# Second pair of heads turned and compared while the first pair's clusters are found, and the table of exponentials loaded early

## The chip, the cores and the metric

The kernel runs on one core of a Trainium2 chip. The metric is the device time of one execution in microseconds (us). The kernel before took 892.93 us, the median of four runs (891.25 to 893.72).

## What is computed

Two blocks, one after the other. The first is a routed attention over q, k and v of shape (4, 8, 768, 64): four batches, eight heads, 768 rows, 64 columns. Each row of q and of k is assigned to one of 16 clusters, whose centroids are given for each head, and a query sees only the keys of its own cluster:

```
q_assign = argmax(q_n @ c_n)              # over 16 clusters; k_assign likewise
mask   = q_assign[..., :, None] == k_assign[..., None, :]
scores = where(mask, q @ k.T / sqrt(64), -1e9)
attn   = softmax(scores)
x      = attn @ v                         # then (batch, row) x (head, column): 3072 x 512
```

The second block is a mixture of experts: each of the 3072 rows of x goes to the one of eight experts with the largest logit of `x @ w_gate`, through `relu(x @ w1[e]) @ w2[e]` (512 to 1024 to 512), and the result is scaled by the softmax weight of the chosen expert. Everything is in float32.

## The kernel before, in words

The attention works on 16 groups, each of them a pair of heads of one batch; group 0 is the first pair, group 1 the second. For one group the steps are functions of the kernel:

- `load` (L506): SyncE issues five transfers, two for q, two for k, one for v. q and k have two buffers each, v has three.
- `turn` (L570): TensorE turns q and k, 12 transposes of 128 x 128, eight in the first piece and four in the second, each piece into one PSUM tile of the ring `sps` (three tiles). VectorE scales q out of PSUM (L582), then ScalarE copies what k there is (L583), and later the second piece (L585).
- `similar` (L587): TensorE compares all rows with the centroids (L592, eight matmul instructions into the single PSUM tile `mps`, four of them on q and then four on k), and ScalarE copies the result out (L597). `similar2` (L599) turns it back with three transposes (L603), and ScalarE copies it out (L605).
- `assign` and `assign2` (L607, L616): the largest of 16, with ties going to the first: VectorE (L611, L612), GpSimd (L613), VectorE (L619, L620).
- `put` (L625): TensorE turns the one-hot rows (L630, 12 transposes in bfloat16, again into a tile of `sps`); ScalarE copies those of q out (L634), then VectorE those of k (L635).
- `score` (L645), 12 for a group: two products of q and k (L652) with the product of the one-hot rows added to them in PSUM (L655), which drives the scores of other clusters far down; ScalarE takes the exponential (L657), and VectorE adds up the sums for the softmax (L660, L664).
- `attend` (L666), 12 for a group: the exponentials times v (L672), summed up in the PSUM tile `O`.

`finish`, `weigh`, `x_turn`, `gate` and `keep_rows` then make the rows of x and the logits. The experts follow at the end; a few of their steps are begun during the attention.

The order on every engine is written out by hand: each engine runs its instructions strictly in the order in which the program issues them. That order is set by turns. In turn n the program issues three scores, then the jobs entered for (n, 0), then the three attends of the turn before, then the jobs for (n, 1). A group has four turns (TG = 4). The line `at(n - 4, 0, turn, g, 0)` and those after it (L776 to L782) enter a group's preparation in the four turns ahead of its first score, n = 4g. So group 0 is prepared in turns -4 to -1, in which there is no score, and group 1 in turns 0 to 3, beside the scores of group 0.

Before all this, at L519 to L565, the centroids and the gate's weights are loaded on ScalarE's queue, groups 0 and 1 on SyncE's queue (L522, L523), and the centroids are normalised: ScalarE squares them (L544) and takes a root (L546), VectorE and TensorE do the rest. A function of ScalarE that isn't in the table at hand is preceded by a load of another table. GpSimd makes constants there, and more of them in turn 1 (`place_consts`, L358).

Of the kernel before, what the change touches and what calls it, by code (L numbers as in the profile page):

```python
# [12 lines left out]
AF = mybir.ActivationFunctionType  # L13
# [170 lines left out]
def kernel(  # L184
# [11 lines left out]
    nc = tc.nc  # L196
# [4 lines left out]
    HP = H // 2  # L201
# [28 lines left out]
    def fetch(e, i):  # L230
        i %= 3
        w1 = wpools[i].tile([P, DB, F], F32, name=f"w1_{i}")
        w2 = wpools[i].tile([P, FB, Dm], F32, name=f"w2_{i}")
        nc.sync.dma_start(out=w1, in_=moe_w1[bass.ds(e, 1)].rearrange("e (a p) f -> p (e a) f", p=P))
        nc.sync.dma_start(out=w2, in_=moe_w2[bass.ds(e, 1)].rearrange("e (a p) d -> p (e a) d", p=P))
        return w1, w2
# [255 lines left out]
    with ExitStack() as actx:  # L492
# [11 lines left out]
        rows = {}  # L504

        def load(g):  # L506
            b, hp = divmod(g, HP)
            for name, src in (("q", q), ("k", k)):
                t = rows[g, name] = ld.tile([P, NQ, 2, D], F32, name=name + "_in")
                for a in range(2):  # L510
                    nc.sync.dma_start(out=t[:, :, a, :], in_=src[b, 2 * hp + a].rearrange("(p j) d -> p j d", j=NQ))
            t = rows[g, "v"] = ld.tile([P, 2, NQ, D], F32, name="v_in", bufs=3)
            nc.sync.dma_start(
                out=t.rearrange("p a j d -> p a (j d)"),
                in_=v[b, 2 * hp : 2 * hp + 2].rearrange("a (p j) d -> p a (j d)", j=NQ),
            )
# [2 lines left out]
        nc.scalar.dma_start(out=csb, in_=centroids.rearrange("h c d -> (h c) d"))  # L519
        wg_in = consts.tile([P, DB, E], F32)  # L520
        nc.scalar.dma_start(out=wg_in, in_=moe_w_gate.rearrange("(a p) e -> p a e", p=P))
        load(0)  # L522
        load(1)  # L523
        make_identity(nc, ident)
        nc.vector.tensor_copy(ident_b, ident)
        first_c = iota("first_c", [P, C], [[-1, C]], C, 0)
# [15 lines left out]
        csq = consts.tile([P, D], F32)  # L542
        cs2 = consts.tile([P, 1], F32)
        nc.scalar.activation(csq, csb, AF.Square, accum_out=cs2)  # L544
        cnrm = consts.tile([P, 1], F32)
        nc.scalar.activation(cnrm, cs2, AF.Sqrt)  # L546
        cinv = consts.tile([P, 1], F32)
        nc.vector.tensor_scalar_max(cinv, cnrm, 1e-30)
        nc.vector.reciprocal(cinv, cinv)
# [215 lines left out]
        def at(n, part, f, *a):  # L765
            jobs.setdefault((n, part), []).append((f, a))
# [6 lines left out]
        at(1, 1, place_consts)  # L773
        for g in range(NG):
            n = g * TG
            at(n - 4, 0, turn, g, 0)  # L776
            at(n - 4, 1, turn, g, 1)
            at(n - 3, 0, similar, g)
            at(n - 3, 1, similar2, g)
            at(n - 2, 0, assign, g)  # L780
            at(n - 2, 0, assign2, g)
            at(n - 1, 0, put, g)  # L782
            at(n + TH, 1, finish, g, 0)
            at(n + 2 * TH, 1, finish, g, 1)
            if g < NG - 1:
                at(n + TG + 2, 0, weigh, g)
                at(n + TG + 2, 1, weigh2, g)
                at(n + TG + 3, 1, x_turn, g, 0)
                at(n + TG + 4, 0, x_turn, g, 1)
                if g % HP == HP - 1:  # L790
                    at(n + TG + 3, 0, gate, g // HP)
                    at(n + TG + 4, 0, keep_rows, g // HP)
# [39 lines left out]
        n = (NG - HP) * TG  # L832
# [10 lines left out]
        n = NG * TG  # L843
# [8 lines left out]
        for g in range(2, NG):  # L852
            at((g - 2) * TG + 1, 0, load, g)
# [23 lines left out]
    with tc.tile_pool(name="sm", bufs=1) as sm:  # L877
# [21 lines left out]
        for part in parts:  # L899
            n, over = part["n"], part["over"]  # L900
# [84 lines left out]
    with tc.If(nx > XU):  # L985
        with tc.For_i(XU, nx, 1) as i:
# [4 lines left out]
            g = dict(n=[P], rows=N, w=fetch(ex, 0), gi=lambda j: gi[:, 0:1], si=lambda j: gi[:, 1:2], apart=False)  # L991
# [36 lines left out]
```

## Time and profile before

| what | value |
|---|---|
| median of four runs | 892.93 us |
| the profiled execution | 891.28 us, of which its span 889.4 us |
| TensorE matmul busy | 840.0 us (94%) |
| VectorE, ScalarE, GpSimd busy | 316.0, 263.3, 107.7 us |
| mean granted clock of TensorE | 0.984 |
| first matmul of the program | 7.19 us from the span's start |
| first score (L652) | 18.71 us |
| first score of turn 2 | 31.49 us |

The span runs from the first instruction to the last; what the device time has beyond it lies around the program. All times of single instructions are counted from the span's start. The stretch that the change touches is the first 40 us: the load and normalisation of the centroids, then group 0 from its transposes to its first scores, then turns 0 to 3.

In the views, PE is TensorE's matmuls, PEld its loads of weights, DVE is VectorE, ACT is ScalarE, POOL is GpSimd and SP is SyncE. In a row of the timeline stand the start, the duration, the engine, the line, the operation, what is written and what is read, and in brackets how long the engine was idle before and what ended that. A float32 matmul shows as two instructions or more.

### The profile page before, as it was taken

How to read it: one execution, taken by the hardware profiler on the slowest of the kernel's cores; microseconds unless marked ns; L12 is line 12 of the kernel's file. 1: busy time of each engine (PE TensorE's matmuls, PEld its weight loads, DVE VectorE, ACT ScalarE, POOL GpSimd, SP SyncE). 2: the span in 40 equal slices, each digit the busy share in tenths (PEclk: the TensorE clock that was granted, in tenths of full speed). 3: DMA queues.
4: the chain of work that ended last, by engine and by line, in shares of the span. 5: the costliest groups of instructions: out<-in, count | busy, mean ns of one | idle time of the engine just before them, and what ended most of it. 6: DMA issues, size and time to landing. Idle time of an engine off the chain costs nothing.

```text
span 889.4 us, 10764 instructions
## 1 busy us (share of the span) xinstructions
PE 840.0 (94%) x4397; PEld 438.0 (49%) x4397; DVE 316.0 (36%) x559; ACT 263.3 (30%) x401; POOL 107.7 (12%) x165
## 2 busy tenths in 40 slices
PE   4999999999999999999987899999999999999994
PEld 2444454544445454444655645645344444545462
DVE  2555556556555657756252101010101020200000
ACT  3554555455555555554200110110010101001010
POOL 3000000000000000220024120302020302001010
PEclk8999999999999999999998999999999999999998
DMA  7126321372242201210421144423242422313010
GB/s 161 36 55 223 73 54 64 64 242 54 54 125 55 52 21 35 90 37 1 189 84 39 41 163 171 155 111 143 107 145 99 165 96 81 141 67 109 24 37 7
DMA packets 76186, 81.69 MB, mean 92 GB/s; under 512 B 52831, under 2 KB 56927, under 8 KB 75616
## 3 DMA queue, kind: packets, MB, share of 16 engines
q1 hardware_dynamic: 70208, 60.82, 22.2%
q0 software_dynamic: 5248, 20.04, 6.3%
q8 instruction: 37, 0.61, 0.3%
q14 instruction: 21, 0.17, 0.1%
q10 hardware_dynamic: 672, 0.05, 0.1%
HBM read 68.26 MB, written 13.68 MB: 92 GB/s over the span
## 4 chain that ended last, share of the span: by engine, by line
PE 45%; issue 39%; POOL 7%; DVE 5%; ACT 1%; POOLq 0%; ACTq 0%; DVEq 0%
PE sps L652 14%; PE O L672 13%; PE mps L690 3%; PE sps L655 3%; POOL out_dram L307 3%; POOL xg L270 3%; PE sps L292 3%; PE sps L578 3%; DVE T L664 2%; PE sps L733 1%; PE mps L592 1%; PE sps L630 1%; POOL oh_c L459 1%; PE mps L603 1%; PE sps L336 1%
## 5 line engine op out<-in xcount | busy, mean ns | idle before, releaser
L292 PE MATMUL sps<-xgT,w 128*128 128x416 f32 (+2 forms) x640 | 176.8, 437 | 0.7 <-issue 0.7
L657 ACT ACTIVATE A<-sps 128x768 f32<-128x768 f32 x192 | 154.7, 812 | 68.6 <-PE sps L655 67.6
L652 PE MATMUL sps<-qk 64*128 64x384 f32 x768 | 164.4, 503 | 1.4 <-ACT qk L583 1.0
L336 PE MATMUL sps<-w,h_sb 128*128 128x512 f32 x368 | 160.6, 595 | 1.3 <-DVE h_sb L300 0.9
L292 PEld LDWEIGHTS sps<-xgT,w 128*128 128x128 f32 x640 | 112.2, 192 | 67.7 <-issue 50.6
L664 DVE TENSOR_TENSOR T<-T,A 128x768 f32<-128x768 f32 x128 | 122.5, 957 | 49.1 <-ACT A L657 39.4
L672 PE MATMUL O<-A,v_in 128*64 128x384 f32 x768 | 138.0, 494 | 0.0
L300 DVE TENSOR_SCALAR h_sb<-sps 128x416 f32<-128x416 f32 (+2 forms) x34 | 18.7, 550 | 317.9 <-PE sps L292 317.9
L336 PEld LDWEIGHTS sps<-w,h_sb 128*128 128x128 f32 x368 | 69.1, 190 | 92.4 <-issue 90.5
L652 PEld LDWEIGHTS sps<-qk 64*128 64x128 f32 x768 | 68.1, 188 | 36.9 <-issue 32.6
L306 ACT ACTIVATE zo<-sps,xg 128x512 f32<-128x512 f32 (+1 forms) x34 | 23.3, 685 | 204.5 <-PE sps L336 195.5
L672 PEld LDWEIGHTS O<-A,v_in 128*64 128x64 f32 x768 | 49.4, 136 | 69.8 <-issue 68.4
L307 POOL DMA_INDIRECT out_dram<-zo,s_idx x34 | 33.2, 977 | 351.1 <-ACT zo L306 334.0
L655 PE MATMUL sps<-ohT 64*128 64x384 bf16 x384 | 66.2, 324 | 2.2 <-DVE ohT L635 2.2
L302 ACT ACTIVATE h_sb<-sps 128x416 f32<-128x416 f32 (+2 forms) x34 | 16.5, 484 | 166.5 <-DVE h_sb L300 166.5
L660 DVE SCALAR_TENSOR_TENSOR T<-A 128x768 f32<-128x768 f32 x32 | 30.7, 958 | 84.0 <-ACT A L657 84.0
L613 POOL TENSOR_TENSOR sim<-sim,first_c 128x384 f32<-128x384 f32 x16 | 16.0, 997 | 292.6 <-DVE sim L612 292.6
L270 POOL DMA_INDIRECT xg<-x_rows,g_idx x34 | 33.3, 980 | 25.5 <-DVE xe L940 10.8
L655 PEld LDWEIGHTS <-ohT 64*128 64x128 bf16 x384 | 22.2, 94 | 27.3 <-DVE ohT L635 6.0
L280 PE MATMUL sps<-ident,xg 128*128 128x128 f32 (+1 forms) x136 | 18.4, 266 | 11.2 <-DVE xgT L281 11.2
L680 ACT COPY xT<-O 128x384 f32<-128x384 f32 x32 | 15.4, 481 | 31.4 <-PE O L672 31.4
L690 PE MATMUL mps<-T,one_row 128*32 128x384 f32 x128 | 23.7, 492 | 0.0
(190 smaller groups left out, 541.3 us busy)
## 6 DMA issues: line engine op xcount, KB each, us to landing
w<-in_moe_w_dram SPq DMA_DIRECT2D x20, 2048.0 KB, 9.4
x_rows<-x POOLq DMA_DIRECT2D x4, 1548.0 KB, 6.7
q_in<-in_q_dram SPq DMA_DIRECT2D x32, 192.0 KB, 4.5
k_in<-in_k_dram SPq DMA_DIRECT2D x32, 192.0 KB, 4.9
v_in<-in_v_dram SPq DMA_DIRECT2D x16, 384.0 KB, 3.4
xg<-x_rows,g_idx POOLq DMA_INDIRECT x34, 5.0
out_dram<-zo,s_idx POOLq DMA_INDIRECT x34, 3.3
csb<-in_centroids_dram ACTq DMA_DIRECT2D x1, 32.0 KB, 1.7
```

Of the source, the lines that this page charges most:

```text
L270: nc.gpsimd.indirect_dma_start(out=g["xg"][0:m, j, :], out_offset=None, in_=x_d[0 : g["rows"], :], in_offset=bass.IndirectOffsetOnAxis(ap= ...
L292: nc.tensor.matmul(o, lhsT=g["w"][0][:, c, fb * P : (fb + 1) * P], rhs=g["xT"][:, c, :cols], start=(c == 0), stop=(c == DB - 1),)
L307: ins = nc.gpsimd.indirect_dma_start(out=out[:, :], out_offset=bass.IndirectOffsetOnAxis(ap=g["si"](j)[0:m], axis=0), in_=zo[0:m], in_offs ...
L336: nc.tensor.matmul(zp, lhsT=g["h"][:, fb, j * P : (j + 1) * P], rhs=g["w"][1][:, fb, :], start=(fb == 0), stop=(fb == FB - 1),)
L578: nc.tensor.transpose(ps[:, i * P : (i + 1) * P], rows[g, "qk"[w]][:, j].rearrange("p a d -> p (a d)"), ident)
L652: nc.tensor.matmul(ps[:, a, 0:HS], lhsT=qk[g][r, 1, ks], rhs=qk[g][r, 0, qs], start=True, stop=False)
L655: nc.tensor.matmul(ps[:, a, 0:HS], lhsT=ohT[g][r, 1, ks], rhs=ohT[g][r, 0, qs], start=False, stop=True)
L657: nc.scalar.activation(A[u], ps[:, :, 0:HS], AF.Exp)
L660: nc.vector.scalar_tensor_tensor(T[g, half], in0=A[u - 1], scalar=1e-9 / P, in1=A[u], op0=ALU.add, op1=ALU.add)
L664: nc.vector.tensor_tensor(T[g, half], T[g, half], A[u], op=ALU.add)
L672: nc.tensor.matmul(O[g, half][a * D : (a + 1) * D, 0:HS], lhsT=rows[g, "v"][:, a, j, :], rhs=a_[:, a, :], start=(j == 0), stop=(j == NQ - 1),)
L690: nc.tensor.matmul(ps[half * 32 : (half + 1) * 32, 0:HS], lhsT=one_row[:, i, :] if i < 2 else wg[:, g % HP, :], rhs=t[half][:, i, :] if i ...
```

## The change

It has four parts.

1. `load` is split into `load_qk` and `load_v`. For groups 0 and 1 the transfers are issued in the order q and k of group 0, q and k of group 1, v of group 0, v of group 1. The later loads keep their order.
2. After the root of the centroids' norms ScalarE gets one more activation: an Exp of the 128 x 1 norms into a column of `csq` that nobody reads any more.
3. `turn` and `similar` of group 1 are entered in turn -2, after `assign` and `assign2` of group 0, and `similar2` of group 1 in turn -1, after `put` of group 0. They were in turns 0 and 1.
4. `assign`, `assign2` and `put` of group 1 stay in turns 2 and 3, and all other groups stay where they were.

```diff
         def load(g):
+            load_qk(g)
+            load_v(g)
+
+        def load_qk(g):
             b, hp = divmod(g, HP)
             for name, src in (("q", q), ("k", k)):
...
+        def load_v(g):
+            b, hp = divmod(g, HP)
             t = rows[g, "v"] = ld.tile([P, 2, NQ, D], F32, name="v_in", bufs=3)
...
-        load(0)
-        load(1)
+        for f in (load_qk, load_v):
+            for g in range(2):
+                f(g)
...
         nc.scalar.activation(cnrm, cs2, AF.Sqrt)
+
+        nc.scalar.activation(csq[:, 0:1], cnrm, AF.Exp)
...
         for g in range(NG):
             n = g * TG
-            at(n - 4, 0, turn, g, 0)
-            at(n - 4, 1, turn, g, 1)
-            at(n - 3, 0, similar, g)
-            at(n - 3, 1, similar2, g)
+            if g == 1:
+
+                for f, a in ((turn, (g, 0)), (turn, (g, 1)), (similar, (g,)), (similar2, (g,))):
+                    at(-1 if f is similar2 else -2, 1, f, *a)
+            else:
+                at(n - 4, 0, turn, g, 0)
+                at(n - 4, 1, turn, g, 1)
+                at(n - 3, 0, similar, g)
+                at(n - 3, 1, similar2, g)
             at(n - 2, 0, assign, g)
             at(n - 2, 0, assign2, g)
             at(n - 1, 0, put, g)
```

## The prediction

> **What bounds the kernel now.** I read the engine shares and the slices of the page first, then the chain that ended last within the first 40 us, then the timeline and the half-microsecond windows there. The page says that TensorE is busy nearly everywhere:
>
> ```profile
> PE 840.0 (94%) x4397; PEld 438.0 (49%) x4397; DVE 316.0 (36%) x559; ACT 263.3 (30%) x401; POOL 107.7 (12%) x165
> PE   4999999999999999999987899999999999999994
> ```
>
> Only the first slice and the last stand at 4. What shortens the start before the dense part therefore comes off the end one for one, and so does TensorE work that is taken out of the dense part and put into an idle stretch. TensorE's waits after the start are short (the longest is 2.2 us, for oh_c at L459) and none is for a load, so I see nothing later that would swallow a shift. The chain of the first 40 us (start, length, engine, line) shows both sides of the change:
>
> ```profile
> 13.35 0.49 ACT sim L605
> ...
> 16.70 0.57 DVE oh L620
> 17.27 0.05 issue
> 17.32 1.46 PE sps L630 x12
> 18.78 1.58 PE sps L652 x4
> ...
> 25.00 0.88 DVE qk L582
> 25.88 0.02 issue
> 25.90 0.38 ACT qk L583
> 26.28 0.04 issue
> 26.32 0.92 PE sps L652 x4
> ...
> 28.21 0.78 PE mps L592 x8
> 28.99 2.09 PE O L672 x12
> 31.08 0.48 PE mps L603 x3
> 31.55 0.85 PE sps L652 x4
> ```
>
> From 13.3 to 17.3 the cluster choice of group 0 goes through ACT, DVE and POOL and TensorE has nothing: 4.01 us. From 22.83 on it turns and compares group 1 between scores. The timeline adds who waits, in square brackets:
>
> ```profile
> 10.37 0.37 ACT L583 COPY qk<-sps 128x256 f32<-128x256 f32 x1 [5.51 <-DVE qk L582]
> 17.32 1.46 PE L630 MATMUL sps<-ident_b,oh 128*128 128x128 bf16 x12 [4.01 <-DVE oh L620]
> 19.63 1.28 ACT L657 ACT_TABLE_LOAD   x1
> 22.83 0.87 PE L578 MATMUL sps<-ident,q_in 128*128 128x128 f32 x6
> 26.32 0.92 PE L652 MATMUL sps<-qk 64*128 64x384 f32 x4 [0.96 <-ACT qk L583]
> ```
>
> The windows give the granted clock in the third figure from the right:
>
> ```profile
> 14.50:15.00 0.50, 0.00 (x0) 0.00 (x0) 0.50 (x1) 0.00 (x0) 0.00 (x0) 0.85 1.30 216
> 21.50:22.00 0.50, 0.50 (x6) 0.23 (x4) 0.00 (x0) 0.24 (x1) 0.00 (x0) 0.82 0.00 0
> ```
>
> Between them it is 0.50. So it fell at 14.85 (0.7 of that half at full speed), 1.5 us after the last matmul of 13.3, and rose at 21.68: 6.83 us at half speed.
>
> **The change part by part.** I count to one point that is the same in both programs: the start of score 6 (turn 2), at 31.49 before. The rest keeps its order, so its shift is the result.
>
> *What leaves the dense part.* From turns 0 and 1 go the 12 transposes (22.83 to 24.29, 1.46 us), the 0.96 us wait for their PSUM tile to be copied out, the comparison L592 (0.78 in the chain) and the three transposes L603 (0.48): 3.68 us.
>
> *Where it goes.* On TensorE's queue the order becomes: L603 of group 0 (ends 13.31), transposes of group 1, L592 of group 1, the transposes L630 of group 0, L603 of group 1, score 0. The transposes find TensorE idle and the clock still up: 12 x 0.145 (six took 0.87) = 1.75, from 13.35 to 15.1, free. But the copy L582 out of PSUM stands on DVE's queue behind L619 and L620 of group 0, which wait for POOL. It starts when L620 ends, about 17.2 (at 24.92 it overlapped the tail of its predecessor too), takes 0.95 and ends at 18.16. ACT's copy L583 follows it as at 10.37 and 25.90, and L585 ends 0.86 later (10.37 to 11.23): 19.04. L592 of group 1 needs these copies, and **L630 of group 0 is queued behind it on TensorE**. That is the new wait: L630 now waits for a DVE copy of the next group and for eight matmuls, and behind it stand all scores.
>
> *Price of that wait.* The second half of L592 can load at 19.08. In group 0 that half ran at nearly full speed: loads at 11.28, end at 12.18, 0.90 us. For half speed there is no row. Two passes start 0.32 apart at full speed, which makes 0.64 at half: 0.09 + 2 x 0.64 + 0.2 = 1.6 us. So L592 ends at 19.98 or at 20.7; its streaming is over some 0.18 earlier. L630 took 1.46 at half speed, and 0.84 at full speed (at 64.43). Then come ACT's copy L634 (0.04 + 0.80), DVE's L635 (0.03 + 0.56) and 0.05 to the first L655, by the rows at 18.82 and 19.65.
>
> *Which clock.* First-half matmuls of L592 took 849 ns and the last 487 ns, so the clock first rose between 10.5 and 11.7. Steps at 11.44, 14.85, 18.26 and 21.68, one each 3.41 us, fit all three changes (an estimate from these rows). Before, TensorE was busy for about 1.3 of the 3.4 us up to 14.85 and lost the clock; the transposes now fill 13.35 to 14.85, so it should hold there. Up to 18.26 TensorE is busy only until 15.1, so it falls there and returns at 21.68. I take half speed for L592 and L630, as this is nearest to the row at 14.85: streaming over at 20.5, L630 to 21.93, L634 to 22.76, L635 to 23.35, L655 of score 0 at 23.40. Before it was 20.26: 3.14 us late.
>
> The Trainium skill (TensorE: Matmul & The Clock Gate, "What's actually happening") has the array go cold only after a whole idle window of about 3.4 us. By that rule the 3.2 us gap from 15.1 to 18.3 would often cost no clock, and the sum would be that of the first rival below; but the same rule would not have let the clock fall at 14.85, 1.5 us into a gap, so I follow the row.
>
> *What comes back.* Scores 0 and 1 ran at half speed before (L655 at 20.26 and 21.77, 1.51 apart); after 21.68 they run 0.81 apart (43.32, 44.13, 44.94). So L655 of score 5 is at 23.40 + 5 x 0.81 = 27.45, the attends start 0.26 later and take 2.09: score 6 starts at 29.80. ACT keeps up: an exp is 0.81 too, and the PSUM tile of score u is read 0.6 us before score u+3 wants it. **31.49 - 29.80 = 1.69 us gained.** (As a balance: 3.68 out, 3.14 lost at score 0, and some 1.2 of half-speed scores saved.)
>
> *The table.* The 1.28 us load at 19.63 stands before the first exp, but L655 of score 0 ended at 20.76 and the exp began at 20.93: it was worth 0.17 at most, and the next exp waited for TensorE at 22.13 anyway. I take 0; at most 0.17 is gained. The early load and a one-column exp (1.28 + 0.2, from 4.87 to 6.4) lie in ACT's 5.51 us of idleness before 10.37; uncovered they would cost 1.5. Without the move the load would now meet L605 of group 1 on ACT before exp 0, up to 0.8, so it protects the gain rather than adds one.
>
> *SyncE's queue.* The four q and k loads of group 1 pass v of group 0: v's issue goes from 3.61 to about 7.2 (1.23 + 2.40 of issuing), and with some 4.7 us to landing it is there by 12, against 27.7 when it is first read. Group 1's q and k were issued by 8.19 and, at 4.6 to landing, there by 12.8, so they were in time for 13.35 even without the reorder: nothing gained. Group 3's q and k, which waited 10.1 us for the transposes until 23.73, can go at about 14; they are needed late, and v of group 3 waits for the attends in both. POOL's constants (16.0 to 21.0) are not moved.
>
> The profiled execution took 891.28: a span of 889.4 and 1.9 around it. It becomes 889.6. The median of the four runs is 1.65 above it, so on the median I forecast 892.93 - 1.69 = **891.24**. What one measurement can tell from no change is about 0.2%, 1.79 us, so this lies right at the edge.
>
> **The rivals.**
>
> *A, the clock does not fall.* For it: the new gap is 3.2 us instead of 4.0, and where the steps fall against the program need not be the same in each run. Against it: 14.85. L592 then ends at 19.98, L630 runs from 19.8 to 20.65, L655 of score 0 comes at 22.13: 1.27 sooner, 2.96 gained, 889.97.
>
> *B, one more stretch at half speed.* For it: L592 uses 32 columns and may be too little work to raise the clock at 21.68; for other positions of the steps, too, the kernel before would have had one slow score less. Then L630 ends 0.2 later, and scores 0 and 1 are 1.51 apart instead of 0.81: 1.69 - 0.2 - 0.7 = 0.8 gained, 892.1.
>
> *C, slower: half speed until about 32.* One mechanism, at the scores of turns 0 and 1: the clock returns three steps late. L655 of scores 0 to 5 come at 23.5, 25.0, 26.5, 28.0, 29.5 and 31.0, the attends end at 33.9: 2.4 us lost, 895.3. It decides from a return at about 30 on. For it: at 18.26 the clock did not return although TensorE had just started again. Against it: by 21.68 TensorE had been busy without a break and it returned.
>
> *D, the change does nothing.* Only the reorder of loads and the table alone would give this (0 to 0.17); the moved matmuls are queue order and can't be hidden.
>
> **How the numbers follow.** Forecast 0.52, its own range 890.6 to 891.9 (gains of 1.0 to 2.3, for other positions of the clock steps and the bounds of L592): 0.23 of it is over 1.79, 0.29 under. A 0.23, faster. B and D 0.15, same. C 0.10, slower. Faster 0.46, same 0.44, slower 0.10. Left out of the range are C and the outer tenth: it goes from A's 889.97 less 0.4, 889.6, to B's 892.1 plus 1.2, 893.3 (a single run of the kernel before lay up to 1.7 from the median, most of them less than 1).
>
> **What would show it.** Right: transposes of group 1 from 13.35 to 15.1; L582 of group 1 at 17.2, right after L620; L630 near 20.5 with L592 before it; L655 of score 0 near 23.4 and score 6 near 29.8; no table load near 20; a clock of 1.00 at 15 and 0.50 from 18.3 to 21.7. Wrong: L630 still at 17.3, or L655 of score 0 beyond 25.1, where the gain is gone; a later wait of TensorE for a load would refute the one-for-one shift.

## The result

The changed kernel takes 889.56 us, the median of 48 runs, against 892.74 us for the kernel before (76 runs); the ratio is 0.9973, with a 95% interval of 0.9967 to 0.9979. It is faster by 0.27%, some 2.4 us. The two medians are 3.2 us apart; the ratio goes with the means, 892.14 and 889.73. The forecast was 1.69 us (0.19%). On the forecast's own base of 892.93 us the ratio gives 890.5: inside its whole range (889.6 to 893.3), just below the 890.6 to 891.9 of its main case.

The lines of the changed kernel stand lower in the file by 10: the copy out of PSUM L582 is now L592, the comparison L592 is L602, the transposes of the one-hot rows L630 are L640, and L652 and L655 are L662 and L665. In this document score 0 is the first of a group's twelve scores, score 6 the first of turn 2. The page of the changed kernel, engine shares and slices:

```profile
PE 839.5 (95%) x4397; PEld 438.0 (49%) x4397; DVE 315.5 (36%) x559; ACT 263.2 (30%) x402; POOL 107.5 (12%) x165
PE   4999999999999999999987899999999999999994
```

The work is the same; only its place has moved. The timeline of the changed kernel shows the place (start, length, engine, line; in brackets the idle time before and what ended it):

```profile
13.20 0.82 PE L588 MATMUL sps<-ident,q_in 128*128 128x128 f32 x6
13.85 0.82 PE L588 MATMUL sps<-ident,k_in 128*128 128x128 f32 x6
...
16.17 0.55 DVE L629 TENSOR_REDUCE top<-sim 128x24 f32<-128x384 f32 x1 [1.11 <-POOL sim L623]
...
16.75 0.56 DVE L630 TENSOR_TENSOR oh<-sim,top 128x384 bf16<-128x384 f32 x1
...
17.23 0.95 DVE L592 TENSOR_SCALAR qk<-sps 128x768 f32<-128x768 f32 x1
...
18.33 2.29 PE L602 MATMUL mps<-qk,cblk 128*32 128x384 f32 x8 [3.65 <-DVE qk L592]
...
20.55 1.46 PE L640 MATMUL sps<-ident_b,oh 128*128 128x128 bf16 x12
...
23.50 0.34 PE L665 MATMUL sps<-ohT 64*128 64x384 bf16 x2
...
29.89 0.92 PE L662 MATMUL sps<-qk 64*128 64x384 f32 x4
```

The transposes of group 1 fill what was idle. Their copy L592 follows L630 on DVE, the comparison L602 waits for it for 3.65 us, and L640 of group 0, which before ran at 17.32, runs behind L602 at 20.55. The first one-hot product of score 0 (L665) is late by 3.24 us, and score 6 nevertheless starts at 29.89 instead of 31.49: 1.60 us sooner. The windows of the changed kernel date the clock's steps (the third figure from the right; the last two rows are for later):

```profile
14.50:15.00 0.50, 0.17 (x2) 0.00 (x0) 0.50 (x1) 0.00 (x0) 0.00 (x0) 1.00 1.35 221
16.00:17.00 1.00, 0.00 (x0) 0.00 (x0) 0.80 (x2) 0.00 (x0) 0.91 (x6) 1.00 1.12 321
18.50:19.00 0.50, 0.50 (x4) 0.00 (x0) 0.00 (x0) 0.50 (x2) 0.43 (x4) 0.89 1.36 219
22.00:22.50 0.50, 0.50 (x6) 0.28 (x4) 0.00 (x0) 0.45 (x1) 0.00 (x0) 0.70 0.00 0
...
470.00:472.00 2.00, 1.57 (x11) 1.57 (x11) 0.73 (x5) 0.00 (x0) 1.42 (x2) 0.50 0.00 0
774.00:776.00 2.00, 2.00 (x12) 0.39 (x8) 0.00 (x0) 0.00 (x0) 0.00 (x0) 0.50 1.02 422
```

It is at half speed from 18.89 to 22.30, one stretch of 3.41 us where the kernel before had 6.83. One step of 3.41 us before 18.89 lies 15.47, and there it held: at 16 to 17 us it is still 1.00, with TensorE idle.

The shift of 1.6 us is still there at the last token matmul (472.4 before, 470.8 after), but the spans differ by 2.3 us (889.4 and 887.1). The other 0.7 lies behind it, in a stretch that the change doesn't touch. Two windows of the kernel before, at 494 and 626 us:

```profile
494.00:496.00 2.00, 2.00 (x6) 1.43 (x5) 0.00 (x0) 0.00 (x0) 0.00 (x0) 0.50 0.02 4
626.00:628.00 2.00, 2.00 (x12) 0.44 (x12) 0.24 (x1) 0.00 (x0) 0.00 (x0) 0.50 1.03 420
```

The last two windows of the changed kernel above, at 470 and 774 us, are of the same kind. Both kernels run at half speed for a while at the token matmuls (6.8 us before, 10.2 after, which cost the changed kernel 1.1) and in single stretches of 3.4 us among the experts: two before (492.7 to 496.1, 625.8 to 629.2), one after (773.2 to 776.6). One such stretch costs 1.7: from their first matmul to the end of the last the experts take 386.1 us with two and 384.4 with one. Two stretches against one, less the 1.1, make 0.6 of the 0.7.

### The profile page after: what moved, and what is told of

It is laid out like the page before. It is cut to its first block, busy times and chain, and to the rows that moved or that the text cites. A ratio compares the mean times of both kernels' runs of the same rounds, so it can differ in the third digit from the quotient of the medians.

```text
span 887.1 us, 10766 instructions
## 1 busy us (share of the span) xinstructions
PE 839.5 (95%) x4397; PEld 438.0 (49%) x4397; DVE 315.5 (36%) x559; ACT 263.2 (30%) x402; POOL 107.5 (12%) x165
## 4 chain that ended last, share of the span: by engine, by line
PE 46%; issue 39%; POOL 7%; DVE 5%; ACT 1%; DMA 0%; POOLq 0%; ACTq 0%; DVEq 0%
PE sps L662 14%; PE O L682 13%; PE mps L700 3%; PE sps L665 3%; POOL out_dram L307 3%; POOL xg L270 3%; PE sps L292 3%; PE sps L588 3%; PE mps L602 2%; DVE T L674 2%; PE sps L743 1%; PE sps L640 1%; POOL oh_c L459 1%; PE sps L336 1%; PE mps L613 1%
## 5 line engine op out<-in xcount | busy, mean ns | idle before, releaser
L662 PE MATMUL sps<-qk 64*128 64x384 f32 x768 | 162.9, 499 | 0.5 <-DVE x L746 0.5
L662 PEld LDWEIGHTS sps<-qk 64*128 64x128 f32 x768 | 67.7, 186 | 35.9 <-issue 33.2
L665 PE MATMUL sps<-ohT 64*128 64x384 bf16 x384 | 66.0, 323 | 2.3 <-DVE ohT L645 2.0
L665 PEld LDWEIGHTS <-ohT 64*128 64x128 bf16 x384 | 22.1, 94 | 26.8 <-DVE ohT L645 5.7
L292 PE MATMUL sps<-xT,w 128*128 128x128 f32 x192 | 24.6, 295 | 0.0
```

The costliest lines, as they stand in the source:

```text
L292: nc.tensor.matmul(o, lhsT=g["w"][0][:, c, fb * P : (fb + 1) * P], rhs=g["xT"][:, c, :cols], start=(c == 0), stop=(c == DB - 1),)
L662: nc.tensor.matmul(ps[:, a, 0:HS], lhsT=qk[g][r, 1, ks], rhs=qk[g][r, 0, qs], start=True, stop=False)
L665: nc.tensor.matmul(ps[:, a, 0:HS], lhsT=ohT[g][r, 1, ks], rhs=ohT[g][r, 0, qs], start=False, stop=True)
```

## The experiments

In all of them two readings are used. The first is the start of score 6 counted from the first transpose of group 0's similarities (L603 before, L613 after). That removes what comes earlier, since this transpose itself starts anywhere between 12.13 and 13.12 in the eleven experiments, in kernels of both kinds: at 12.59 on average in the eight profiles with the move, at 12.60 in the five without it. It is 18.73 before (31.49 - 12.76) and 17.08 after (29.89 - 12.81). The second is the median.

### One part of the change alone

```diff
# e1: the changed kernel without its loads' order and its early Exp
# e6: the kernel before with only this
+        nc.scalar.activation(csq[:, 0:1], cnrm, AF.Exp)
# e7: the kernel before with only this
-        load(0)
-        load(1)
+        for f in (load_qk, load_v):
+            for g in range(2):
+                f(g)
```

> Only the four functions of group 1 are moved; the loads keep their old order and the table of exponentials is loaded before the first exp as before. Theory 1 (queue account: 3.7 us leave the dense part, 3.1 are lost because L630 of group 0 stands behind L582 and L592 of group 1, 1.2 come back from scores at full speed): the move is the whole gain. The table load falls after the copy of sim on ACT, at about 23.2, so that the first exp comes at 24.5 instead of 23.9, which the PSUM ring hides but for 0 to 0.4 us; score 6 at 29.9 to 30.3, median 889.6 to 890.2. Theory 2 (the table is what counts, 1.28 us on the path): score 6 at 31.2 and a median of 890.9 or more.

> The kernel before with the early Exp alone. Theory 1: the first exp comes 0 to 0.2 us sooner, nothing else moves; equal to the kernel before within 0.2 us. Theory 2 (the table counts 1.28 us): 1.3 us faster.

> The kernel before with q and k of group 1 loaded ahead of v of group 0, alone. Theory 1: nothing waits for these loads; equal to the kernel before within 0.2 us, with score 6 near 31.5. Theory 6 (the first matmul of the program, at 6.68 with the change against 7.19 before, came sooner because of the order of loads): first matmul at 6.7 and 0.5 us faster.

Measured: e1 889.8 us, ratio 0.9981 (0.9967 to 0.9994); e6 891.09, ratio 1.0 (0.9986 to 1.0013); e7 890.98, ratio 0.9998 (0.9984 to 1.0013). Score 6 stands at 29.46, 30.40 and 30.96. The move is the gain. The table's load and the order of the loads, each alone, are not distinguishable from nothing, which ends theory 2; theory 6 ends too, because e7, with the new order of loads, starts its first matmul at 7.17, and e1, with the old one, at 6.87. In e1 the load of the table falls where it was expected (e1's line numbers are lower by 3 than those of the changed kernel):

```profile
22.59 1.28 ACT L664 ACT_TABLE_LOAD   x1
...
23.89 3.62 ACT L664 ACTIVATE A<-sps 128x768 f32<-128x768 f32 x5
...
24.75 0.30 PEld L659 LDWEIGHTS sps<-qk 64*128 64x128 f32 x4 [0.51 <-ACT A L664]
```

The first exp ends later, so score 3 waits for its PSUM tile until 24.75; at the distance of the scores around it, it would have started at 24.63. Its one-hot product also follows 0.75 us after it instead of 0.64. From the one-hot product of score 0 to score 6 e1 takes 6.62 us (22.84 to 29.46) and the changed kernel 6.39, both at full clock, so by these profiles the early table is worth 0.23 us inside the move. That e1 needs 17.08 us from the transpose to score 6 all the same goes with its clock, which came back 0.89 us sooner after the transpose.

e6 and e7 also show what was not expected: counted from the transpose, score 6 comes after 18.07 and 18.28 us, with the same instructions that took 18.73 in the profile before. In both the clock was down for 3.4 us only, not for 6.8. So the start of the kernel before has no single length; the 1.60 of one pair of profiles is 1.0 to 1.65, counted from the transpose, over these three.

### The wait of the one-hot transposes

```diff
# e2: the changed kernel, the comparison of group 1 behind the one-hot transposes of group 0
-                    at(-1 if f is similar2 else -2, 1, f, *a)
+                    at(-2 if f is turn else -1, 1, f, *a)
# e3: instead, the second half of group 0's choice behind group 1's comparison
+                    if f is similar:
+                        at(-2, 1, assign2, 0)
...
-            at(n - 2, 0, assign2, g)
+            if g:
+                at(n - 2, 0, assign2, g)
```

> As the changed kernel, but L592 of group 1 stands behind L630 of group 0 on TensorE instead of ahead of it. Theory 1: L630 runs at 17.4 instead of 20.55; ACT's copy of it waits behind the two copies L593 and L595 of group 1 until 19.1, so the first L665 comes at 22.1 (after L602 of group 1 and its transposes, which still stand ahead of score 0), 1.4 us sooner than 23.50; median 888.2. Theory 3 (the wait of L640 is not what delays score 0, as ACT and DVE would be late anyway): no gain over the changed kernel, 889.6.

> As the changed kernel, but the second half of the cluster choice of group 0 (L619 and L620 of the kernel before) is entered after the move of group 1, so that DVE copies group 1's q out of PSUM while GpSimd multiplies, instead of behind it. Theory 1: the copy runs from 15.0 to 16.0 in DVE's idle 1.1 us, L602 of group 1 from 16.1 to 17.7, L640 of group 0 at 17.6 at full speed, the first L665 at 19.9 instead of 23.50, score 6 at 26.3 instead of 29.9; median 886.0. Theory 3 (DVE's order is not the cause of the delay): the first L665 within 0.5 us of 23.5, median 889.6.

In e2 L640 starts at 16.89, at once after the cluster choice, and the first L665 at 22.00 (22.1 expected). Score 6 comes 16.05 us after the transpose, 1.03 less than in the changed kernel. The twelve executions fall apart, six at 885.7 to 887.8 and six at 891.4 to 894.3, so that the median, 889.55, says nothing; the ratio is 0.998 (0.9958 to 1.0002). The trace shows the wait removed; the times don't show a gain.

In e3 the copy runs on DVE while GpSimd multiplies:

```profile
14.93 0.95 DVE L592 TENSOR_SCALAR qk<-sps 128x768 f32<-128x768 f32 x1
...
16.02 1.64 PE L602 MATMUL mps<-qk,cblk 128*32 128x384 f32 x8 [1.40 <-DVE qk L592]
16.12 0.55 DVE L629 TENSOR_REDUCE top<-sim 128x24 f32<-128x384 f32 x1 [0.25 <-POOL sim L623]
...
17.59 0.84 PE L640 MATMUL sps<-ident_b,oh 128*128 128x128 bf16 x12
...
19.92 0.34 PE L665 MATMUL sps<-ohT 64*128 64x384 bf16 x2 [0.23 <-DVE ohT L645]
```

DVE's wait for GpSimd falls from 1.11 to 0.25 us, L602 is nearly over when L640 wants the array, and TensorE's gap shrinks to 1.40 us, so that the clock never falls: L602 takes 1.64 and L640 0.84. Score 6 starts at 26.31 (26.3 expected), 13.54 us after the transpose, 3.54 less than with the change. The median is 886.58 (886.0 expected), the ratio 0.9946 (0.9927 to 0.9964). Theory 3 is out: the place of one DVE copy in its queue is what held score 0 up. The 3.54 us hold two things, since the shorter gap also keeps the clock up: 1.26 is the clock by e5 below, and the other 2.28 (15.82 - 13.54, both at full clock) the place in the queue.

### The clock at the start

```diff
# both: n transposes of the identity into a PSUM tile that nobody reads
+        def spin(n):
+            ps = wide().rearrange("p a c -> p (a c)")
+            for i in range(n):
+                nc.tensor.transpose(ps[:, i % 8 * P : (i % 8 + 1) * P], ident, ident)
# e4: the kernel before
+        at(-2, 1, spin, 26)
# e5: the changed kernel
-                for f, a in ((turn, (g, 0)), (turn, (g, 1)), (similar, (g,)), (similar2, (g,))):
+                for f, a in ((turn, (g, 0)), (turn, (g, 1)), (spin, (19,)), (similar, (g,)), (similar2, (g,))):
```

> The kernel before, with 26 transposes of the identity added on TensorE between 13.3 and 17.1, into a PSUM tile that nobody reads, so that only the clock changes. Theory 1: the clock stays at full speed; L630 takes 0.84 instead of 1.46, scores 0 and 1 follow each other after 0.81 instead of 1.51 except where the table load holds the first exp; score 6 at 30.2 instead of 31.49, median 891.4 (1.3 less). Theory 4 (the whole gain of the change is the clock that its transposes keep up): score 6 at 29.9 and a median of 889.6, as with the change itself. Theory 5 (transposes do not count as work for the clock): no change, 892.7, with the clock at 0.50 from 14.9 on.

> The changed kernel, with 19 transposes of the identity added on TensorE between the transposes of group 1 and L602 of group 1 (15 to 18 us), into a PSUM tile that nobody reads. Theory 1 (half speed for L602 and L640 is a term of the loss at score 0, as forecast in rival A): the clock stays at 1.00, L602 takes 1.64 instead of 2.29, L640 0.84 instead of 1.46, the first L665 comes at 22.1 instead of 23.50 and score 6 at 28.6 instead of 29.89; median 888.2. Theory 4 (the clock at the start is not on the path, as the copies of ACT and DVE are late anyway): score 6 unmoved, 889.6.

The timeline of e5:

```profile
14.44 2.24 PE L776 MATMUL sps<-ident 128*128 128x128 f32 x19
...
18.27 1.64 PE L602 MATMUL mps<-qk,cblk 128*32 128x384 f32 x8 [1.60 <-DVE qk L592]
...
19.85 0.84 PE L640 MATMUL sps<-ident_b,oh 128*128 128x128 bf16 x12
...
22.17 0.34 PE L665 MATMUL sps<-ohT 64*128 64x384 bf16 x2 [0.23 <-DVE ohT L645]
```

The clock is 1.00 from 11.73 on through the whole start, the first L665 comes at 22.17 (22.1 expected), score 6 at 28.56, 15.82 after the transpose. Half speed had cost the changed kernel 17.08 - 15.82 = 1.26 us. The median is 888.57, the ratio 0.9967 (0.9954 to 0.9981).

In e4 score 6 comes 17.61 us after the transpose, so half speed had cost the kernel before 0.46 to 1.12 in the three profiles of its kind. At 30.73 it misses the expected 30.2: score 4 still waits 1.13 for the copies of group 1 out of PSUM, which I had not carried over. The median is 890.84, the ratio 0.9995 (0.998 to 1.0009). Theory 5 is out, as the clock stays at 1.00 on transposes alone; theory 4 is out as well: keeping the clock up in the kernel before does not give what the change gives. At full clock on both sides the change is worth 17.61 - 15.82 = 1.79 us, which is the order of the queues (and the early table) without the clock.

### The stretches beyond 470 us

```diff
# e8: e3, and a filler of five after each row tile at the experts' borders
# e9, e10, e11: e4, e5 and e3, and a filler of five only where j is even
+            if spins and j % 2 == 0 and j + 1 < len(g["n"]):
+                sp = ps_m.tile([P, 512], F32, name="mps")
+                for i in range(spins):
+                    nc.tensor.transpose(sp[:, i % 4 * P : (i % 4 + 1) * P], ident, ident)
# all four: 13 ahead of the 2nd, 3rd and 4th quarter of the token matmuls
+            if n == NT and t and t % (n // 4) == 0:
+                sp = wide()
+                for i in range(13):
+                    nc.tensor.transpose(sp[:, 0, i % 4 * P : (i % 4 + 1) * P], ident, ident)
```

> The kernel of e3, with transposes of the identity added in later idle spots of TensorE: 13 ahead of each of the last three quarters of the token matmuls (L469), and 5 after the turn of each of the experts' row tiles. Theory 7 (what the profiles show beyond 470 us: single stretches of 3.4 us at half speed at the experts' borders, some in one execution and some in the next, 1.7 us each, and 10.2 us at half speed around 465, make the executions of one kernel fall into groups): these stretches vanish, the executions lie in one group within about 1 us, the median is 2 to 4 us below that of e3. Theory 8 (the groups come from elsewhere, such as the weights' transfers): groups as before, 2 to 3 us apart, and the median no lower than that of e3.

e8 took 887.48 us, ratio 0.9946 (0.9929 to 0.9963), no less than e3. The stretches ahead of the last matmul are gone but for one, at 488 us, right after a wait of TensorE of 2.21 us that was 0.67 in e3; the mean clock is 0.993 against 0.986, and six executions lie between 886.11 and 887.69. But the fillers cost what they save. In e8 the border at 618 (the turning of an expert's rows) reads:

```profile
618.44 0.60 PE L280 MATMUL sps<-ident,xg 128*128 128x128 f32 x4
618.88 0.71 PE L284 MATMUL mps<-ident 128*128 128x128 f32 x5
619.89 0.66 PE L280 MATMUL sps<-ident,xg 128*128 128x128 f32 x4 [0.30 <-DVE xgT L285]
620.38 0.71 PE L284 MATMUL mps<-ident 128*128 128x128 f32 x5
620.93 0.60 PE L280 MATMUL sps<-ident,xg 128*128 128x128 f32 x4
```

The second filler stands where there was no wait. From the first transpose to the next matmuls the border takes 4.23 us, against 3.84 in e3. Theory 7 holds for the stretches, which vanish but for one, and failed on the price; on the groups e11 below goes against it.

> The kernel of e4 (that before, with transposes of the identity in the start's gap), with identity transposes also in the later idle spots: 13 ahead of each of the last three quarters of the token matmuls and 5 only where TensorE waits at the experts' borders (not after every row tile, as in e8). So the clock should stay up nearly everywhere and only the order of the queues is left to differ from e10. Theory 7: executions in one group within about 1 us, mean clock 0.993 or more. Score 6 near 30.7, as in e4.

> The kernel of e5 (the changed one, with transposes of the identity in the start's gap), with the same later additions as e9. Theory 1 (the queue account, at full clock): score 6 near 28.6, 2.2 us ahead of e9, and the median lower than that of e9 by the same 2.2 us, as nothing later swallows a shift. Theory 4 (the change gains through the clock alone): no difference between e9 and e10.

> The kernel of e3 with the later additions of e9. In e8 the additions after each row tile held TensorE up by 0.4 us at each border, 10 borders; without those that meet no wait: Theory 7: median 883.5 (e8's 887.5 less 4), executions in one group. Theory 8 (the additions gain nothing, whatever their place): 886.6 or more, as e3.

Measured: e9 888.51 us, ratio 0.9955 (0.994 to 0.9971), executions from 887.46 to 888.73; e10 887.61, ratio 0.9945 (0.9929 to 0.9961), from 886.67 to 888.03; e11 884.33, ratio 0.9911 (0.9893 to 0.9929), from 882.65 to 886.02. From the transpose score 6 comes after 17.61, 15.82 and 13.54 us, to the hundredth as in e4, e5 and e3.

e10 is 0.9 us below e9 and not 2.2. In the two profiles score 6 stands at 29.74 and 28.89, so 0.85 apart, and the spans are 886.5 and 885.6; from score 6 to the experts' first matmul they take 461.31 and 461.29. What shift there is arrives at the end in full. That it is 0.85 and not 1.79 lies ahead of the transpose, which started at 12.13 in e9 and 13.07 in e10: the comparison of group 0 took 1.64 there and 2.17 here, the difference between a clock that had risen early and late, and the first matmul started at 6.61 and 7.02. The other executions bear the small difference out: the means of six each are 0.90 us apart, with a 95% interval of 0.3 to 1.5, so 1.79 did not arrive in these times. By the mean granted clock the executions of e10 are at half speed for 1.8 us more than those of e9, which may be part of the rest; no run settles it. The expected 2.2 was wrong in itself: it was 30.73 - 28.56, from two profiles without taking out the start.

e11 is the fastest version, 0.89% below the kernel before (883.5 us had been expected). Its executions still spread over 3.4 us, as those of e3 do, although the fillers are in: that it would leave one group did not come true. TensorE waits 2.76 us ahead of the first expert there (2.82 in e9, 2.77 in e10), so part of what the token matmuls gained is lost to a wait that no run resolved.

## Why the prediction was right

**The order of the queues** was right in each of its steps, on the profiled pair:

| step | forecast | measured |
|---|---|---|
| copy of group 1's q ends on DVE | 18.16 | 18.18 |
| comparison of group 1 ends | 20.7 | 20.62 |
| one-hot transposes of group 0 | 20.5 to 21.93 | 20.55 to 22.01 |
| first L655 (now L665) | 23.40 | 23.50 |
| score 6 | 29.80 | 29.89 |
| gained there | 1.69 | 1.60 |

The transposes of group 1 took 1.47 us and not 1.75, which changed nothing, as their copy waits for DVE. The decisive reading was that the copy L582 stands behind L620 on DVE, and L630 behind L592 on TensorE (lines of the kernel before). e2 took away the second and e3 the first, and score 6 came 1.03 and 3.54 us sooner, the latter with the clock's 1.26 in it.

**The clock** was right in kind. It held once, as the transposes kept TensorE busy, and it fell at the next step. But the forecast took the steps' places from the profile before (14.85 and 18.26), and in the measured execution they lay at 15.47 and 18.89. That the half-speed stretch still covered the comparison and the one-hot transposes is luck in part: in e1, with the same order, it ended at 20.98, before the one-hot transposes were over (20.13 to 21.36). Rival A's price for a clock that doesn't fall, 1.27, is e5's 1.26. Rival A itself didn't come about in the profiled execution, nor did B or C. On the rule of the Trainium skill (TensorE: Matmul & The Clock Gate, "What's actually happening") that a whole idle window is needed, the measurements decide against it: the clock fell at 625.8 in the kernel before although TensorE's matmuls had been busy for about half of the 3.4 us before (1.62 us), with waits of 0.84 and 0.94 us:

```profile
623.45 1.09 PE L280 MATMUL sps<-ident,xg 128*128 128x128 f32 x8 [0.84 <-DVE xgT L281]
625.48 0.43 PE L280 MATMUL sps<-ident,xg 32*128 32x32 f32 x4 [0.94 <-DVE xgT L281]
```

**The table and the loads** were worth about the forecast 0 to 0.2: no difference in the times of e6 and e7, 0.23 us by the profile of e1. The loads' own figures hold too: group 3's q is issued at 14.05, as forecast.

**What was mis-sized** is the sum for the median. The forecast took one profile's start for the kernel's start, and held that nothing behind it depends on the program's shift. The mean of the 71 executions of the kernel before whose clock is on record is 892.11, that of 50 of the changed kernel 889.71: 2.40 us apart. The start gives 1.0 to 1.65 of that, by the three profiles of the old order against the 17.08 of the new one (e1 has the same 17.08). The other 0.75 to 1.4 lies behind the start or is an effect of which profiles are at hand. By the mean granted clock of each execution (time at half speed = 2 x (1 - clock) x span) it was at half speed for 29.2 us before and 26.8 after; in the two profiles 7.5 and 8.1 us of that lie behind the last matmul, where they cost nothing. Among the 71 a microsecond more at half speed goes with 0.32 us more of time, which makes 0.8 for the 2.4. That is an association, and the half-speed time of the start is in it, so it can't simply be added to the start's share: the sum is not closed.

In part, then, the forecast was near by luck: the start that it counted on was the slowest of the three profiles of the old order, and what lies behind the start, which it put at nothing, added to the gain (0.7 us in the profiled pair, for a half-speed stretch fewer among the experts, less the 1.1 at the token matmuls). The stretches are part of what spreads the executions: e8, e9 and e10, with the fillers, range over 1.6, 1.3 and 1.4 us (six executions each), the kernel before over 4.1 (eleven, beside e9 and e10). But e11, with the same fillers as e9, ranges over 3.4, so they are not shown to be all of it. Of the kernel before 33 of the 71 lie above 892 us, of the changed kernel none of 50. Why the changed kernel spends less time at half speed on average was not settled. Their place differs from execution to execution, and a dozen profiles are too few for the pattern.

## What to carry to other kernels

Work moved into an engine's idle stretch is not free if its result has to pass through another engine's queue: look for the copy that follows it, see what that copy is queued behind, and put it where that engine waits anyway (here 3.5 us for a change of place, 1.26 of it by the clock). A gap on TensorE can cost twice, once as the gap and once as a half-speed stretch that follows (3.65 us of waiting in the changed kernel, and 1.26 for the clock), and fillers paid here only in spots where TensorE waits (e8 against e11). Where executions of one kernel spread by more than the gain that is sought, count from an event close to the change in several profiles; one pair mixes the change with the position of the clock's steps.

## What the runs showed of the hardware

The clock's steps lie on one grid of 3.413 us for a whole execution: in the profile before, the falls at 14.85 and 468.83 are 133 such steps apart, and in the changed kernel those at 18.89 and 466.03 are 131. The grid's offset differs from profile to profile. In all thirteen profiles the clock fell only at the end of such a step in which TensorE's matmuls had been busy for 57% of the time or less, and it held only where they had been busy for 48% or more. So it didn't take an idle step to lose it, and between the two figures the busy share doesn't decide.

The experts' borders, 20 to 52 us apart, catch a step in some profiles and not in others, at 1.7 us each. The mean clock goes with the time but doesn't set it: in the kernel before 0.986 stands at 890.0 to 890.9 us in 21 of 22 executions and 0.980 or 0.981 at 892.9 to 894.2, but 0.984 at 890.9 to 891.8 in thirteen and at 893.9 to 894.6 in seven. What these seven spend was not found; the one profile of that kernel, at 891.28, is none of them.

Transposes of the identity alone keep the clock at 1.00 (e4: from 12.45 to 15.86 TensorE ran nothing but transposes, and the clock held).
